# Strassen's scheme for six of seven feature blocks of a spatial product

## The chip, the cores and the metric

The kernel runs on one core of one Trainium2 chip. The metric is device time in microseconds, the median of several executions. The core has five engines with a queue of instructions each: TensorE (PE in the profile, its weight loads PEld), VectorE (DVE), ScalarE (ACT), GpSimd (POOL) and SyncE (SP), which here issues nearly all DMAs.

## The reference

One block of a network: an attention part A, then a gated MLP part B, each with a modulated layer norm ahead and a gated residual behind.

```python
def _B_ref(x, w_in, w_sp, b_sp, w_out):       # x: 1 x 2048 x 448, F = 1792, Fh = 896
    z = _gelu(jnp.einsum('bsd,df->bsf', x, w_in))
    z1 = z[..., :Fh].copy()
    z2 = _layernorm(z[..., Fh:], axis=-1)
    g = jnp.einsum('ts,bsf->btf', w_sp, z2) + b_sp[None, :, None]    # w_sp: 2048 x 2048
    return jnp.einsum('bsf,fd->bsd', z1 * g, w_out)
...
h = _layernorm(x, axis=-1) * (1 + ca) + sa
x = x + ga * _A_ref(h, A_wqkv, A_w_phi, A_wo)
h = _layernorm(x, axis=-1) * (1 + cb) + sb
x = x + gb * _B_ref(h, B_w_in, B_w_sp, B_b_sp, B_w_out)
```

The change concerns the product `w_sp @ z2`, a 2048 x 2048 by 2048 x 896 product, called the spatial product here. Inputs and outputs are bf16; matmuls add up in f32.

## The kernel before

The kernel is a list of small steps. A string, `ORDER`, names them one after the other, and a loop at the end of `fast_path` calls each. Each engine works through its own instructions in that order; nothing rearranges them, so the order by hand sets every queue. A word such as `gM:0,3@A2` calls the step `gM` with arguments 0 and 3 and gives it the PSUM slot A2; `zN:15/G` gives `zN` the engine GpSimd (V is VectorE, S ScalarE, Y SyncE). A second path, `general_path`, is taken only for extreme inputs, by a flag that `guard` computes; it does not run here.

PSUM has eight banks. Before the change they are five slots of a pool: A0, A1 and A2 of two banks, B0 and B1 of one.

The sequence has 2048 rows, 16 tiles (`NT`) of 128. The 896 features are seven blocks of 128 (`FC`). The steps of the last third, around the change:

- `zM` (matmul, L990), `zG` (gelu on ScalarE, L994), `zQ` (squares), `zR` and `zW` (moments, inverse root), `zN` (L1012) make the normalised `z2n`, sequence on the partitions, features in the free dimension.
- `yM` (matmul, L1018) and `yG` (gelu on ScalarE, L1021) make `z1T`, features on the partitions, for a chunk of 512 rows and one feature block.
- `W` (L1026) loads one eighth of a chunk of `w_sp`, transposed by DMA, issued on SyncE. Four chunks of 512 output rows each; their buffers are `wsp0`, the two halves of `EQ` (before that the attention's exponentials) and `hT` (before that the transposed hidden rows).
- `gM` (L1034) is the spatial product: for a chunk and a feature block, 16 matmuls with a 128 x 128 tile of `z2n` as weights and a slice of the chunk as the moving operand, into one bank. The last chunk is cut in two, of 384 and 128 columns:

```python
CH = [(0, 0, 512), (1, 0, 512), (2, 0, 512), (3, 0, 384), (3, 384, 512)]
```

- `gG` (L1040, L1041) takes the bank on VectorE: it adds the bias into an f32 buffer, then multiplies with `z1T` in place.
- `oM` (L1047) is the output product of one tile of 128 rows, seven matmuls over the feature blocks; `oE` (L1050) adds the residual; `oD` (L1053) issues the output DMA on SyncE.
- `wts` (L907) scales a block of `w_out` by the gate, on GpSimd. `guard` (L1056 to L1062) reduces two tables for the flag.

In `ORDER` the 35 units of `gM` stand in line from the last `yM` on; four `yM` and the `oM` of finished chunks stand among them.

Of the kernel before, what the change touches and what calls it, by code (L numbers as in the profile page):

```python
# [515 lines left out]
W:1,7 yG:3,6 gM:0,2@B0 W:1,5 yG:1,6 gG:0,5 gM:0,4@A1 gG:0,2 gG:0,3 yM:2,6@B0 gG:0,4 gM:0,6@A2 yG:2,6 wts:5/G yM:1,3@B0 gG:0,6 gM:0,1@A1 gM:1,4@A2
gM:1,1@A0 gG:1,4 wts:3/G gG:0,0 W:2,0 gM:1,0@A2 yG:1,3 gG:1,1 gM:1,5@B0 W:2,7 gG:1,0 gM:1,6@B1 gG:1,5 gG:0,1 gM:1,2@B0 gG:1,6 wts:4/G W:2,4 W:2,5
wts:6/G gM:1,3@B1 gG:1,2 gM:2,2@B0 gG:1,3 guard@A2 oM:4,0,7@B1 gG:2,2 gM:2,4@A2 oM:1,0,7@B0 oM:0,0,7@A1 oM:5,0,7@A0 oE:0 oE:1 gM:2,1@A1 oD:0/Y gG:2,4
oD:1/Y oM:2,0,7@B0 oM:3,0,7@A2 oE:2 oD:2/Y oM:7,0,7@B0 oE:3 oE:4 oD:3/Y yM:2,1@A2 oE:5 oD:4/Y oD:5/Y yM:2,3@B1 yG:2,1 gM:2,0@A0 gG:2,1 yG:2,3 W:3,6
W:3,7 W:3,0 oM:6,0,7@B1 gG:2,0 W:3,3 gM:2,5@A2 oE:6 oE:7 W:3,2 W:3,1 gM:2,6@B0 oD:6/Y gG:2,5 W:3,4 W:3,5 gM:2,3@B1 gG:2,6 gM:3,2@B0 read gG:2,3  # L520
oM:9,0,7@B1 gG:3,2 oM:11,0,7@A2 gM:3,3@B0 gM:3,4@A1 gG:3,3 gM:3,5@B0 gG:3,4 gM:3,6@A1 gG:3,5 oM:8,0,7@B0 gG:3,6 gM:3,1@A0 oE:8 oE:9 oD:8/Y oD:9/Y
gM:3,0@B0 gG:3,1 oD:7/Y gM:4,6@B1 gG:3,0 gM:4,3@A1 gG:4,6 oM:13,0,7@B0 gG:4,3 gM:4,0@B1 gM:4,5@A1 gG:4,0 gM:4,1@A0 gG:4,5 oM:10,0,7@B1 gG:4,1
gM:4,2@A1 oE:10 oE:11 oM:12,0,7@A0 oD:10/Y gG:4,2 oD:11/Y gM:4,4@B1 hint oE:12 oE:13 oM:14,0,7@A2 oD:12/Y gG:4,4 oD:13/Y oM:15,0,6@B0 oE:14 oD:14/Y
oM:15,6,7@B0 oE:15 oD:15/Y
"""


def fast_path(tc, A_x, A_wqkv, A_w_phi, A_wo, B_w_in, B_w_sp, B_b_sp, B_w_out, c, w_mod, out, flag):
# [525 lines left out]

    def guard(slot):
        nc.vector.tensor_reduce(out=flg[:, 0:1], in_=ksum[:].rearrange("p i a h -> p (i a h)"), axis=AX.X, op=ALU.max)  # L1056
# [96 lines left out]
```

## Time and profile before

| | us |
|---|---|
| median of 3 runs | 266.69 |
| lowest and highest run | 265.77, 266.75 |
| span of the profiled execution, first to last instruction | 264.7 |
| the spatial product's stage in it, first gM matmul to the last oM | 138.75 to 260.62 |

The span is that of one profiled execution. That execution's own time is not listed apart; the span is 2.0 us below the median, which is what lies around it in a run. A row of a group gives line, engine, operation, output and inputs, shapes, count, then busy time, mean duration of one in ns, and the idle time of the engine just before, with what ended it. A row of the timeline begins with the start in us from the first instruction and the duration.

### The profile page before, as it was taken

The numbers are of one execution on the slowest core, as the hardware profiler recorded it, in microseconds if no ns is written. First come the engines' busy times: TensorE is split into PE (matmuls) and PEld (weight loads), VectorE is DVE, ScalarE is ACT, GpSimd is POOL, SyncE is SP. The second block draws the span as 40 slices with busy tenths as digits, with TensorE's granted clock in tenths as the row PEclk, the third lists the DMA queues.
The fourth block names the chain that finished last, engine by engine and source line by source line (L and its number), as shares of the span: only waits on it lengthen the run. The fifth ranks groups of instructions, "written<-read, shape, count | busy, mean of one in ns | idle before, by whom it ended". The sixth has DMA issues, their size and how long they took to land.

```text
span 264.7 us, 4376 instructions
## 1 busy us (share of the span) xinstructions
PE 255.1 (96%) x1645; PEld 138.4 (52%) x1653; DVE 159.1 (60%) x389; ACT 113.1 (43%) x238; POOL 67.5 (26%) x93
## 2 busy tenths in 40 slices
PE   7899999999699999989999999999999999999993
PEld 5764566665445555545444444444444444555771
DVE  5799999966987978867610262435623534335562
ACT  2689978759859998889772000000000100000000
POOL 6328672368623543223362000000000000000000
PEclk9999999999989999999999999999999999999998
DMA  7994999700599431891892000000001398000012
GB/s 179 276 278 102 170 240 276 226 2 20 109 171 156 105 80 40 177 144 41 184 166 49 0 0 0 2 0 0 0 5 35 99 189 120 0 0 23 32 38 78
DMA packets 68656, 25.23 MB, mean 95 GB/s; under 512 B 58129, under 2 KB 68498, under 8 KB 68626
## 3 DMA queue, kind: packets, MB, share of 16 engines
q1 hardware_dynamic: 67088, 22.72, 42.6%
q10 hardware_dynamic: 1538, 2.15, 3.2%
q8 instruction: 15, 0.25, 0.4%
q14 instruction: 15, 0.12, 0.1%
HBM read 8.87 MB, written 1.84 MB: 40 GB/s over the span
## 4 chain that ended last, share of the span: by engine, by line
PE 84%; ACT 5%; DVE 5%; DMA 3%; issue 1%; ACTq 0%; DVEq 0%
PE g_ps L1034 36%; PE o_ps L1047 8%; PE z_ps L990 7%; PE z_ps L1018 7%; PE q_ps L890 5%; PE k_ps L842 4%; PE v_ps L850 4%; PE x_ps L950 4%; PE kvacc L873 3%; PE num L918 2%; DMA f_oT<-f_opad 2%; DMA f_wq_raw<-in_A_wqkv_dram 2%; DVE f_t L934 2%; ACT f_junk L962 1%; PE sh_ps L758 1%
## 5 line engine op out<-in xcount | busy, mean ns | idle before, releaser
L1034 PEld LDWEIGHTS <-f_z2n 128*128 128x128 bf16 x560 | 50.4, 98 | 47.7
L1040 DVE TENSOR_TENSOR f_gb<-g_ps,f_bsp 128x512 f32<-128x512 f32 (+2 forms) x35 | 20.4, 582 | 58.9 <-PE g_ps L1034 58.7
L1034 PE MATMUL g_ps<-f_Eq,f_z2n 128*128 128x512 bf16 x219 | 48.7, 379 | 0.3
L1021 ACT ACTIVATE f_z1T<-z_ps 128x512 bf16<-128x512 f32 x28 | 16.2, 596 | 71.9 <-PE z_ps L1018 71.8
L1018 PE MATMUL z_ps<-f_hT,f_win 113*128 113x512 bf16 (+1 forms) x112 | 26.4, 379 | 0.0
L990 PE MATMUL z_ps<-f_win,f_hT 112*128 112x448 bf16 (+1 forms) x128 | 26.1, 352 | 0.0
L1034 PE MATMUL g_ps<-f_hT,f_z2n 128*128 128x384 bf16 (+1 forms) x224 | 25.4, 272 | 0.0
L1034 PE MATMUL g_ps<-f_wsp,f_z2n 128*128 128x512 bf16 x109 | 24.5, 379 | 0.2
L1047 PE MATMUL o_ps<-f_wout,f_z1T 128*128 128x448 bf16 x112 | 22.8, 353 | 0.0
L1041 DVE TENSOR_TENSOR f_z1T<-f_gb,f_z1T 128x512 bf16<-128x512 f32 (+2 forms) x35 | 20.5, 585 | 1.9 <-ACT f_z1T L1021 0.5
L990 PEld LDWEIGHTS <-f_hT 112*128 112x128 bf16 (+1 forms) x128 | 12.3, 97 | 11.8
L856 DVE TENSOR_REDUCE f_ksum<-f_E 128x32 f32<-128x896 bf16 x16 | 16.8, 1067 | 0.8 <-ACT f_E L845 0.6
L1018 PEld LDWEIGHTS <-f_win 113*128 113x128 bf16 (+1 forms) x112 | 10.7, 97 | 12.3
L1050 DVE TENSOR_TENSOR f_xpad<-o_ps,f_x 128x448 bf16<-128x448 f32 x16 | 9.3, 619 | 13.0 <-PE o_ps L1047 12.5
L895 ACT ACTIVATE f_Eq<-q_ps 112x1024 bf16<-112x1024 f32 x16 | 16.0, 1034 | 2.7 <-PE q_ps L890 2.7
L934 DVE TENSOR_TENSOR f_t<-num,f_w 128x896 bf16<-128x896 f32 x16 | 16.7, 1083 | 0.2
L994 ACT ACTIVATE f_z2g<-z_ps 128x896 bf16<-128x896 f32 x16 | 14.6, 914 | 3.6 <-PE z_ps L990 3.5
L845 ACT ACTIVATE f_E<-k_ps 128x448 bf16<-128x448 f32 x32 | 15.4, 555 | 1.6 <-PE k_ps L842 0.9
L950 PE MATMUL x_ps<-f_wo,f_oT 112*128 112x448 bf16 x64 | 15.5, 372 | 0.7 <-DMA f_oT<-f_opad 0.7
L1047 PEld LDWEIGHTS <-f_z1T 128*128 128x128 bf16 x112 | 10.7, 98 | 9.4
L890 PE MATMUL q_ps<-f_hT,f_Wq 113*128 113x512 bf16 (+1 forms) x64 | 14.9, 378 | 0.0
L842 PE MATMUL k_ps<-f_Wk,f_hT 113*128 113x448 bf16 (+1 forms) x64 | 14.1, 352 | 0.0
(157 smaller groups left out, 337.8 us busy)
## 6 DMA issues: line engine op xcount, KB each, us to landing
out_dram<-f_xpad SPq DMA_DIRECT2D x16, 112.0 KB, 1.7
f_x<-in_A_x_dram SPq DMA_DIRECT2D x3, 448.0 KB, 9.6
f_wm<-in_w_mod_dram SPq DMA_DIRECT2D x3, 406.0 KB, 6.3
f_wout<-in_B_w_out_dram SPq DMA_DIRECT2D x1, 784.0 KB, 7.7
f_wmg<-in_w_mod_dram SPq DMA_DIRECT2D x2, 392.0 KB, 5.0
f_win<-in_B_w_in_dram SPq DMA_DIRECT2D x1, 784.0 KB, 8.3
f_win<-in_B_w_in_dram ACTq DMA_DIRECT2D x1, 784.0 KB, 8.9
f_bsp<-in_B_b_sp_dram ACTq DMA_DIRECT2D x1, 512.0 KB, 5.3
```

The lines of the kernel that those rows point to most:

```text
L842: nc.tensor.matmul(t[:, 0, 0:D], lhsT=hT[0:KR[m], i, m, :], rhs=Wk[0:KR[m], m, :], start=(m == 0), stop=(m == KC - 1))
L856: nc.vector.tensor_reduce(out=ksum[:, i], in_=Er[i % NR][:].rearrange("p s (c f h) -> p (s c) h f", c=4, h=HP), axis=AX.X, op=ALU.add)
L890: nc.tensor.matmul(t[:, u, :], lhsT=Wq[0:KR[m], m, cc * CB:cc * CB + P], rhs=hT[0:KR[m], 4 * st:4 * st + 4, m, :], start=(m == 0), stop=(m ...
L934: nc.vector.tensor_tensor(out=tr[i % 2][:], in0=numv(i)[:, :, :, 0:DH], in1=wr[i // 2 % 2][:, i % 2].unsqueeze(3).to_broadcast([P, 2, H, D ...
L950: nc.tensor.matmul(t[:, 0, 0:D], lhsT=oT[0:CB, i % 4, cc, :], rhs=wo_s[0:CB, cc, :], start=(cc == 0 and not with_x), stop=(cc == KC - 1))
L990: nc.tensor.matmul(t[:, hf, 0:D], lhsT=hT[0:KR[m], i, m, :], rhs=win_s[0:KR[m], m, FH + hf * D:FH + (hf + 1) * D], start=(m == 0), stop=(m ...
L1018: nc.tensor.matmul(t[:, 0, :], lhsT=win_s[0:KR[m], m, fc * P:(fc + 1) * P], rhs=hT[0:KR[m], 4 * st:4 * st + 4, m, :], start=(m == 0), stop ...
L1021: nc.scalar.activation(out=stage_b()["z1T"][:, fc, st * 512:(st + 1) * 512], in_=ps["y%d_%d" % (st, fc)][:, 0, :], func=ACT.Gelu_apprx_tanh)
L1034: nc.tensor.matmul(g[:, 0, 0:b - a], lhsT=later["z2n"][:, s_, fc * P:(fc + 1) * P], rhs=wspT[t][:, s_, a:b], start=(s_ == 0), stop=(s_ == ...
L1040: nc.vector.tensor_tensor(out=gb, in0=ps["G%d_%d" % (ch, fc)][:, 0, 0:b - a], in1=bsp[:, t * TCHF + a:t * TCHF + b], op=ALU.add)
L1041: nc.vector.tensor_tensor(out=z, in0=gb, in1=z, op=ALU.mult)
L1047: nc.tensor.matmul(ps["o" + str(t)][:, 0, 0:D], lhsT=later["z1T"][:, fc, t * P:(t + 1) * P], rhs=wout_s[:, fc, :], start=(fc == 0), stop=( ...
```

## The change

For feature blocks 0 to 5 the spatial product is computed by one level of Strassen's scheme (in Winograd's form). The 2 x 2 blocks are: of `w_sp`, two chunks of 512 output rows by two halves of the sequence (A); of `z2n`, two halves of the sequence by two groups of three feature blocks (B). For each of two pairs of chunks, `p`, and each of three block pairs, `f`, seven products of eight matmuls take the place of eight. Feature block 6 keeps `gM` and `gG`.

New steps:

- `tT` (VectorE, bf16, 128 x 768): the four differences of the B blocks, in quarters, 16 in all. Three go into new views, one over `z2n` itself.
- `sS` (VectorE, bf16, 128 x 2048): the four sums of the A blocks of a pair, in halves, 16 in all.
- `pM`: one product, eight matmuls over 512 columns into one bank. Products 2, 3 and 4 add onto the bank of an earlier one (2 on 1, 4 on 7, 3 on 5), after that has been read.
- `pc` (ScalarE) copies product 1 out; `pb` (GpSimd, two operations) adds the two bias rows to it; `uB`, `uA`, `uW`, `cA` (VectorE, 128 x 512, a bank plus an f32 buffer or the bias) build the four result blocks; `cX` (VectorE or GpSimd) multiplies a result with `z1T` in place.

Moved: chunk 1's `W` loads go where chunk 2's stood; chunk 2 is loaded into the memory of `win_s` and `wo_s` after the last `yM`; chunk 3 into chunk 1's buffer, issued after products 4 of pair 0 have been issued. Four `yM`, the four late `wts` and `zN:15` (now on VectorE) come ahead of the first `gM`. Eight `oM` stand between products 2 and 6 of pair 1; the other eight at the end. `guard` gives its matmul to a new step `guard2`. PSUM is one tile of eight banks, and a slot is a view of it; several SBUF tiles (`win_s` and `wo_s`, `opad` and `oT`, `junk` and `junk2`, the `f_t` and `f_z2g` rings) become views of one tile each.

```diff
+tT:1,0,2/V tT:2,0,2/V tT:3,0,2/V tT:4,0,2/V zQ:12/S yM:1,6@A1 zQ:13/V zM:14@A0 yG:2,0 zR:12,14 ...
+tT:1,2,4/V ... tT:4,2,4/V yM:3,5@A2 W:1,5 yG:1,6 yG:3,6 yG:3,2 yM:2,2@A0 zR:14,16 yG:3,5 yM:3,0@B1 zW:14,16 yG:2,2 zN:14/V zN:15/V
+yM:3,1@A2 ... yG:2,3 wts:5/G wts:3/G wts:4/G wts:6/G W:2,0 W:2,1 W:2,2 W:2,3 W:2,4 W:2,5 W:2,6 W:2,7
+gM:0,6@3 sS:0,1,0/V sS:0,2,0/V gM:1,6@7 sS:0,1,1/V sS:0,2,1/V pM:0,0,1@6 pc:0,0 pb:0,0 gG:0,6 pM:0,1,1@5 pc:0,1 pb:0,1 gG:1,6 pM:0,0,2@6 sS:0,3,0/V
+sS:0,3,1/V pM:0,2,1@1 pc:0,2 pb:0,2 cA:0,0,11 pM:0,1,2@5 cX:0,0,11/G pM:0,2,2@1 cA:0,1,11 cX:0,1,11/G cA:0,2,11 cX:0,2,11/G pM:0,0,6@0 uB:0,0 uA:0,0
+pM:0,0,7@2 uW:0,0 pM:0,1,6@4 uB:0,1 uA:0,1 pM:0,0,4@2 cA:0,0,21 pM:0,1,7@3 uW:0,1 sS:0,4,0/V cX:0,0,21/G pM:0,2,6@7 uB:0,2 uA:0,2 pM:0,1,4@3 cA:0,1,21
...
+sS:1,2,1/V oM:2,0,7@0 oE:2 oD:2/Y sS:1,3,0/V oM:3,0,7@4 oE:3 oD:3/Y sS:1,3,1/V oM:4,0,7@3 oE:4 oD:4/Y oM:5,0,7@6 oE:5 oD:5/Y oM:6,0,7@0 oE:6 oD:6/Y
+oM:7,0,7@4 oE:7 oD:7/Y sS:1,4,0/V pM:1,0,6@0 uB:1,0 uA:1,0 pM:1,0,7@2 uW:1,0 pM:1,1,6@4 uB:1,1 uA:1,1 pM:1,0,4@2 cA:1,0,21 pM:1,1,7@3 uW:1,1
...
+    psum = psp.tile([P, 8, 512], F32, name="f_psum")
+    SLOT = {"A0": (0, 2), "A1": (2, 4), "A2": (4, 6), "B0": (6, 7), "B1": (7, 8)}
+    SLOT.update({str(k): (k, k + 1) for k in range(8)})
     def bank(slot, name):
-        if slot[0] == "A":
-            return psp.tile([P, 2, 512], F32, name=name, tag=slot, bufs=1)
-        return psp.tile([P, 1, 512], F32, name=name, tag=slot, bufs=1)
+        a, b = SLOT[slot]
+        return psum[:, a:b, :]
...
-    wspT = [wsp0[:], EQ[:, 0, :].rearrange("p (n t) -> p n t", t=TCHF), EQ[:, 1, :].rearrange("p (n t) -> p n t", t=TCHF),
-            hT[:].rearrange("p n k t -> p n (k t)")]
+    wspT = [wsp0[:], EQ[:, 0, :].rearrange("p (n t) -> p n t", t=TCHF), wbig[:, 0:NT * TCHF].rearrange("p (n t) -> p n t", t=TCHF),
+            EQ[:, 0, :].rearrange("p (n t) -> p n t", t=TCHF)]
...
+    def tT(k, a, b, eng):
+        z = [[zblk(s, g)[:, a:b] for g in range(2)] for s in range(2)]
+        t1, t2, t4 = [TS[u][:, a:b] for u in range(3)]
+        out_, in0, in1 = {1: (t1, z[0][1], z[0][0]), 2: (t2, z[1][1], t1), 3: (z[0][1], z[1][1], z[0][1]), 4: (t4, z[1][0], t2)}[k]
+        eng.tensor_tensor(out=out_, in0=in0, in1=in1, op=ALU.subtract)
...
+    def sS(p, k, h, eng):
+        A, S = [[v[:, :, h * 256:(h + 1) * 256] for v in w] for w in wblk(p)]
+        out_, in0, in1, op = {1: (S[0], A[2], A[3], ALU.add), 2: (S[1], S[0], A[0], ALU.subtract),
+                              3: (S[2], A[0], A[2], ALU.subtract), 4: (S[3], A[1], S[1], ALU.subtract)}[k]
+        eng.tensor_tensor(out=out_, in0=in0, in1=in1, op=op)
+    PSTART = {1: True, 2: False, 3: False, 4: False, 5: True, 6: True, 7: True}
+    def pM(p, f, k, slot):
+        A, S = wblk(p)
+        a = {1: A[0], 2: A[1], 3: S[3], 4: A[3], 5: S[0], 6: S[1], 7: S[2]}[k]
+        b = {1: zblk(0, 0), 2: zblk(1, 0), 3: zblk(1, 1), 4: TS[2], 5: TS[0], 6: TS[1], 7: zblk(0, 1)}[k]
+        t = ps["P%d_%d_%d" % (p, f, k)] = bank(slot, "p_ps")
+        for j in range(NH):
+            nc.tensor.matmul(t[:, 0, :], lhsT=b[:, j, f * P:(f + 1) * P], rhs=a[:, j, :], start=(PSTART[k] and j == 0), stop=(j == NH - 1),
+                             skip_group_check=True)
...
+    def pc(p, f):
+        nc.scalar.copy(out=slotA(f), in_=pP(p, f, 1))
+    def pb(p, f):
+        nc.gpsimd.tensor_tensor(out=slotB(f), in0=slotA(f), in1=bias(p, 1), op=ALU.add)
+        nc.gpsimd.tensor_tensor(out=slotA(f), in0=slotA(f), in1=bias(p, 0), op=ALU.add)
+    def vadd(out_, bank_, other):
+        nc.vector.tensor_tensor(out=out_, in0=bank_, in1=other, op=ALU.add)
+    def uB(p, f):
+        vadd(slotB(f), pP(p, f, 6), slotB(f))
+    def uA(p, f):
+        vadd(slotA(f), pP(p, f, 6), slotA(f))
+    def uW(p, f):
+        vadd(slotC(f), pP(p, f, 7), slotB(f))
...
```

More of the change, by code (lines that the diff above doesn't have):

```diff
@@ L516 @@
[L516 to L523, printed above, removed]
@@ L549, in fast_path @@
     hT = persist.tile([P, NT, KC, P], BF, name="f_hT")
-    win_s = persist.tile([P, KC, 2 * FH], BF, name="f_win")
-    wo_s = persist.tile([P, KC, D], BF, name="f_wo")
+    wbig = persist.tile([P, KC * (2 * FH + D)], BF, name="f_win")
+    win_s = wbig[:, 0:KC * 2 * FH].rearrange("p (k n) -> p k n", k=KC)
+    wo_s = wbig[:, KC * 2 * FH:].rearrange("p (k n) -> p k n", k=KC)
     wout_s = persist.tile([P, FC, D], BF, name="f_wout")
@@ L559, in fast_path @@
     xpad = persist.tile([P, NX, KC, P], BF, name="f_xpad")
-    opad = persist.tile([P, NO, KC, P], BF, name="f_opad")
+    oo = persist.tile([P, 2 * NO * KC * P], BF, name="f_oo")
+    opad, oT = [oo[:, u * NO * KC * P:(u + 1) * NO * KC * P].rearrange("p (t k e) -> p t k e", t=NO, k=KC) for u in range(2)]
     wsp0 = persist.tile([P, NT, TCHF], BF, name="f_wsp0")
@@ L1004, in stage_b @@
             later["z1T"] = zp.tile([P, FC, S], BF, name="f_z1T")
-            later["z2g"] = [zp.tile([P, 2, D], BF, name=f"f_z2g{r}") for r in range(NZ)]
+            zt = zp.tile([P, NZ * FH], BF, name="f_z2g")
+            later["z2g"] = [zt[:, r * FH:(r + 1) * FH].rearrange("p (a d) -> p a d", a=2) for r in range(NZ)]
+            tmps.extend(f32v(zt[:, u * 1024:(u + 1) * 1024]) for u in range(4))
             later["gb"] = [zp.tile([P, TCHF], F32, name=f"f_gb{r}") for r in range(2)]
@@ L1053, in oD, with zblk @@
         eng.dma_start(out=outv[t], in_=later["ot"][t % NX])
-    def guard(slot):
+    def zblk(s, g):
+        return later["z2n"][:, s * NH:(s + 1) * NH, g * FB:(g + 1) * FB]
+    def tT(k, a, b, eng):
[3 more added lines that the diff above has]
+        eng.tensor_tensor(out=out_, in0=in0, in1=in1, op=ALU.subtract)
@@ new lines, in vadd, with cA @@
+    def vadd(out_, bank_, other):
[6 more added lines that the diff above has]
+        vadd(slotC(f), pP(p, f, 7), slotB(f))
+    def cA(p, f, k):
+        if k == 11:
+            vadd(later["gb"][f % 2][:], pP(p, f, 2), bias(p, 0))
+        elif k == 21:
+            vadd(slotB(f), pP(p, f, 4), slotB(f))
+        elif k == 22:
+            vadd(slotC(f), pP(p, f, 5), slotC(f))
+        else:
+            vadd(slotA(f), pP(p, f, 3), slotA(f))
@@ L1056, in guard, with cX @@
+    def cX(p, f, k, eng):
+        src = {11: lambda: later["gb"][f % 2][:], 21: lambda: slotB(f), 22: lambda: slotC(f), 12: lambda: slotA(f)}[k]()
+        fc, t = f + (3 if k % 10 == 2 else 0), 2 * p + (k // 10 - 1)
+        z = later["z1T"][:, fc, t * TCHF:(t + 1) * TCHF]
+        eng.tensor_tensor(out=z, in0=src, in1=z, op=ALU.mult)
+    def guard():
         nc.vector.tensor_reduce(out=flg[:, 0:1], in_=ksum[:].rearrange("p i a h -> p (i a h)"), axis=AX.X, op=ALU.max)
```

62 lines of the change are left out of this document (50 added, 12 removed).

## The prediction

> **What bounds the kernel now.** I read the page first: who is busy, and whether the clock is full.
>
> ```profile
> PE 255.1 (96%) x1645; PEld 138.4 (52%) x1653; DVE 159.1 (60%) x389; ACT 113.1 (43%) x238; POOL 67.5 (26%) x93
> ...
> PEclk9999999999989999999999999999999999999998
> ```
>
> TensorE is the bound by share. An average over stages does not say what a change in one stage is worth, so next the table by stretches, for the spatial product (columns: stretch, length, then busy us and count of PE, PEld, DVE, ACT, POOL; clock; DMA share; GB/s).
>
> ```profile
> 170.00:180.00 10.00, 9.95 (x47) 4.47 (x46) 5.17 (x9) 0.00 (x0) 0.00 (x0) 1.00 0.00 0
> ...
> 220.00:230.00 10.00, 10.00 (x53) 5.07 (x52) 3.97 (x7) 0.00 (x0) 0.00 (x0) 1.00 0.39 49
> ```
>
> In the stage PE never waits, at full clock; DVE is half idle, ACT and POOL wholly. So here every matmul removed shortens the run, until one of the others is late. The chain of waits in order of time (start, us, what) gives the price of one matmul as chain time, the pipeline overlap taken out:
>
> ```profile
> 131.81 6.94 PE z_ps L1018 x32
> 138.75 0.22 PE g_ps L1034
> ...
> 156.88 3.46 PE g_ps L1034 x16
> ...
> 230.79 10.40 PE g_ps L1034 x64
> ...
> 250.82 2.68 PE g_ps L1034 x48
> ...
> 257.94 2.66 PE o_ps L1047 x14
> ...
> 260.62 0.62 DVE f_xpad L1050
> ```
>
> A matmul over 512 columns costs 3.46/16 = 0.216 us, over 384 columns 10.40/64 = 0.1625, over 128 columns 2.68/48 = 0.056, an o_ps one 2.66/14 = 0.19. The spatial stage runs from 138.75 to 260.62 with no gap.
>
> **PE: what goes.** Before, gM makes 21 units of 16 at 512, 7 of 16 at 384 and 7 of 16 at 128 columns (L1028 splits the last chunk). After, feature block 6 alone keeps gM: 3, 1 and 1 units. The six other blocks are 2 chunk pairs x 3 block pairs x 7 products x 8 = 336 matmuls at 512. So 512-column matmuls go from 336 to 336 + 48, the narrower ones from 112 to 16 each: +48 x 0.216 - 96 x 0.1625 - 96 x 0.056 = 10.4 - 15.6 - 5.3 = -10.6 us (48 of 384 full-width equivalents, one eighth). The o_ps and z_ps matmuls are the same, four yM only stand earlier. If nothing waits, the span of 264.7 becomes 254.1.
>
> **What DVE gets.** Rows of the groups by form (engine, operation, out<-in, count | busy, mean ns | idle before):
>
> ```profile
> L1041 DVE TENSOR_TENSOR f_z1T<-f_gb,f_z1T 128x512 bf16<-128x512 f32 x21 | 14.5, 692 | 1.4 <-ACT f_z1T L1021 0.5
> L1040 DVE TENSOR_TENSOR f_gb<-g_ps,f_bsp 128x512 f32<-128x512 f32 x21 | 14.5, 689 | 44.2 <-PE g_ps L1034 44.1
> L1050 DVE TENSOR_TENSOR f_xpad<-o_ps,f_x 128x448 bf16<-128x448 f32 x16 | 9.3, 619 | 13.0 <-PE o_ps L1047 12.5 <-DMA out_dram<-f_xpad 0.5
> L863 DVE TENSOR_TENSOR f_phik<-f_E,f_kr 128x896 bf16<-128x896 bf16 x12 | 7.2, 627 | 0.1
> L964 DVE SCALAR_TENSOR_TENSOR f_junk<-f_z2g 128x896 bf16<-128x896 bf16 x4 | 4.3, 1086 | 1.1 <-ACT f_z2g L994 1.1
> L907 DVE TENSOR_TENSOR f_wout<-f_wout,f_g_rep 128x448 bf16<-128x448 bf16 x1 | 0.4, 384 | 0.0
> L907 POOL TENSOR_TENSOR f_wout<-f_wout,f_g_rep 128x448 bf16<-128x448 bf16 x6 | 6.1, 1028 | 0.0
> L863 POOL TENSOR_TENSOR f_phik<-f_E,f_kr 128x896 bf16<-128x896 bf16 x4 | 7.1, 1779 | 9.1 <-DVE f_kr L860 8.4 <-ACT f_Eq L895 0.7
> L1056 DVE TENSOR_REDUCE f_flg<-f_ksum 128x1 f32<-128x512 f32 x1 | 0.7, 680 | 0.0
> ```
>
> L907 and L863 on DVE give bf16 tensor_tensor a slope of (627-384)/448 = 0.54 ns per element; L964, another operation with two bf16 inputs, takes 1086 ns for 896, twice that slope. The new operations are plain tensor_tensor, so I take the first: sS, 2048 elements, 627 + 1152 x 0.54 = 1.25 us; tT, 768 elements, 0.56. The other end is L964's: 1.09 + 1152 x 1.04 ns = 2.3 and 0.95. Each evacuation (uA, uB, uW, cA) has the form of L1040, each cX on DVE that of L1041: 0.69, with the gap 0.73. On POOL 512 elements cost, between its rows, 1.14 us.
>
> Now the two queues side by side, because the products accumulate on banks that DVE reads in between, so a late DVE stops PE within a product or two.
>
> ```profile
> 133.83 1.21 ACT L1021 ACTIVATE f_z1T<-z_ps 128x512 bf16<-128x512 f32 x2
> 135.13 0.51 DVE L1012 TENSOR_SCALAR f_z2n<-f_z2g,f_zm,f_zv 128x896 bf16<-128x896 bf16 x1 [0.81 <-POOL f_zv L976]
> ...
> 149.15 0.69 DVE L1040 TENSOR_TENSOR f_gb<-g_ps,f_bsp 128x512 f32<-128x512 f32 x1 [13.50 <-PE g_ps L1034]
> ```
>
> Lead-in (timeline). DVE ends its last normalisation at 135.6 and idles 13.5 us. The 16 tT (9 us) go there and into its smaller gaps before, half of them ahead of the statistics of the last tiles: these eight are 4.7 us with gaps, and as some fall into idle time I put the last zN 3.4 later, near 139 (at most at 140.3), and the last tT 4.7 on, near 143.7. PE starts gM at 138.75 + four yM of 0.867 = 142.2, and I add 0.7: yG:1,6 and yG:3,6 now stand ahead of yG:3,2 on ACT, which ends at 133.83 + 3 x 0.60 = 135.6, while yM:3,0, which wants its bank, is due at 131.81 + 4 x 0.867 = 135.3, plus the hand-over (0.3 to 1.0). So PE starts at 142.9 and last wants zN:15 3 us later: covered.
>
> Pair 0, first part. PE: two gM and six products of 8 matmuls (1.73 each), 6.9 + 10.4, to 160.2; then product 6, which needs sS:1 and sS:2, product 7 with sS:3. DVE from 143.7: four sS 5.1, two gG 2.9, two sS 2.5: S2 is ready at 149, S3 at 154. Covered by 8 us and more. Second part: 15 products, 25.9 us on PE. DVE: 18 evacuations 13.1, six cX 4.4, two sS 2.5, guard 1.9 (two reductions like L1056 and three small ones) = 21.9. Fits, 4 us to spare. Product 4 goes onto product 7's bank and waits for uW, with one product between: 0 to 1.2, I take 0.3, as DVE has slack.
>
> Pair 1, first part. PE: six products 10.4 and eight oM 10.6 = 21. DVE: six sS 7.6, three cA 2.2, eight oE 5.2 = 15. The sS wait for chunk 3, whose DMAs stand on SP behind the last read of chunk 1:
>
> ```profile
> 209.51 8.03 SPq L1026 DMA_TRANSPOSE f_hT<-in_B_w_sp_dram  x6
> ...
> f_hT<-in_B_w_sp_dram SPq DMA_TRANSPOSE x8, 3.8
> ```
>
> Six issues take 8.03, so 1.34 each, landing 3.8 after issue; five products (8.7 us) lie between that read and pair 1. The first four have landed 3 x 1.34 + 3.8 = 7.8 us on, all eight after 13.2, 4.5 us into pair 1: early enough, and the output DMAs behind them on SP lose nothing that PE wants. Chunk 2, into the former win_s, has all of pair 0. Four of the oM have an sS beside their oE, 1.9 us of DVE for 1.32 of PE: 2.4 us behind; the next three oM regain 0.67 each, so oE:6, whose bank product 6 wants, is late by some 0.6 (0 to 2.4). Second part as in pair 0: 13.1 + seven cX 5.1 + two sS 2.5 + two oE 1.3 = 22 of 25.9. POOL has 23 operations of 1.14, 26 us of 90, and ACT six copies; the four wts moved ahead are hidden there. The end (last oM, oE, DMA) is unchanged.
>
> **The sum.** -10.6 + 0.7 + 0.3 + 0.6 and 0.5 for POOL meeting DVE (below) = -8.5. The span goes to 256.2. The time of the profiled execution itself is not listed; its span is 2.0 below the median of the runs, 266.69, so I carry the difference over: 258.2 us. The views of banks and tiles move no work; the built program has 27 more semaphore instructions on DVE and 18 on ACT. Such a one takes 21 ns:
>
> ```profile
> L907 DVEq EVENT_SEMAPHORE  x1: 21/21/21, 55.2 to 55.2; - x1
> ```
>
> All of DVE's on the path would be 27 x 0.021 = 0.6 us; beside the slack above I count none.
>
> **Rivals.** *A: POOL holds DVE.* Where they met:
>
> ```profile
> 54.73 3.16 POOL L907 TENSOR_TENSOR f_wo<-f_wo,f_g_rep 112x448 bf16<-112x448 bf16 x3 [4.31 <-ACT f_g_rep L904]
> ...
> 55.31 0.70 DVE L907 TENSOR_TENSOR f_wo<-f_wo,f_g_rep 112x448 bf16<-112x448 bf16 x1
> ...
> L940 DVE TENSOR_TENSOR f_opad<-f_t x11: 379/382/625, 69.2 to 111.4; 128x448 bf16<-128x448 bf16 x11
> ```
>
> Under POOL's run the DVE operation took 0.70 against 0.384, and the longest of L940 0.625 against 0.382: 0.2 to 0.3 us for one meeting. In the forecast most of these fall into slack. If instead DVE lost the whole POOL operation, then in pair 1's first part nine of them add up to 10.3 to DVE's 15 against PE's 21: 4.3 late, and some 1.5 in each second part, where 3 or 2 are left (22 + 3.4 = 25.4 of 25.9): 7.3 in place of 0.5, 265.0. The Trainium skill, SBUF — State Buffer, "Who interferes with whom", says that a DVE instruction with two SBUF inputs contends with a GpSimd one that reads SBUF and the later one fully blocks; by that rule it would be this case. The trace agrees that they meet, and shows less than a full block.
>
> *B: DVE becomes the bound*, on the slower side. If sS and tT run at L964's slope, 16 x 1.05 + 16 x 0.39 = 23 us more on DVE. Pair 0: the last tT at 150, S3 at 150 + 9.2 + 2.9 + 4.6 = 167 where PE wants it at 161.9: 5 late, and the three cA behind it make the first uB, uA, uW late by 1.5 more. Pair 1's first part then holds 15 + 6.3 = 21.3 plus the wait for chunk 3 against 21, with the oE in step behind an sS of 2.3: 4 to 5 late, and the second parts (24 of 25.9) have nothing left to win back. 5 + 1.5 + 4.5 and the 2.1 above are 13: 266.7 - 10.6 + 13 = 269, slower. It decides where an sS takes over about 2 us. Against it: L863 and L907 are the same operation.
>
> *C: it doesn't save what it says*, because the products wait for each other in the bank chain 6-7-4, one product of 1.73 apart: half of the 1.2 above, 0.6, for each of the six times that a product 4 follows a product 7, is 3.6 in place of 0.3: 261.5, inside the range.
>
> **Chances.** Forecast 0.62 (256.1, with no waits, to 260.5), C 0.10, A 0.12, B 0.12, anything else 0.04. A change under 0.5% (1.3 us) can't be told from none. Of A, 0.06 stays faster, 0.05 is the same and 0.01 slower; of the rest half is faster. Faster: 0.62 + 0.10 + 0.06 + 0.02 = 0.80; same 0.05; slower: 0.12 + 0.01 + 0.02 = 0.15. The range runs from 255.8 (no waits, less a little spread) to 265.0, A's price; B, the upper half of A and half of the rest are left out, 0.20.
>
> **What would show it.** Right: 336 product matmuls at 0.216 in the chain, over 95% PE from the first gM to the end, sS at 1.25, DVE busy 75 to 85% in the stage, end of PE near 252. Wrong: PE waiting on the evacuations for over 5 us in total, sS rows over 1.6 (A or B, by whether a POOL row lies beside them), or PE idle ahead of the first product.

## The result and the profile after

The changed kernel takes 258.06 us (median of four runs, 257.26 to 258.41) against 266.23 for the kernel before, a ratio of 0.969 (95% interval 0.966 to 0.972): 8.2 us, 3.1%, faster. The forecast was 258.2. A second set of runs gave 257.63 against 266.24, 0.967 (0.963 to 0.970).

The head of the page and the clock row, after:

```profile
PE 243.3 (95%) x1501; PEld 127.2 (50%) x1509; DVE 193.9 (76%) x417; ACT 116.9 (46%) x244; POOL 98.1 (38%) x115
...
PEclk9999999999999999999999999999999999999999
```

1501 matmul records in place of 1645; PE is still the bound, with 95% of a shorter span. VectorE has gone from 60% to 76%. The chain of waits in order of time (start, us, what) shows the stage:

```profile
135.95 7.10 PE f_psum L1042 x32
143.05 0.22 PE f_psum L1058
...
196.80 10.59 PE f_psum L1071 x56
...
242.96 7.96 PE f_psum L1071 x42
250.94 0.62 DVE f_xpad L1074
```

From the first gM at 143.05 to the last oM at 250.94 the chain stays on PE; one matmul of `guard2` and some gaps of 0.05 us stand among the products. That is 107.9 us. Before, the same work took 260.62 - 138.75 - 3.47 (the four yM that have moved) = 118.4. The difference is 10.5 us, the 10.6 of the prediction. The first gM starts 0.85 later than its counterpart before (142.2), and 4.5 us of the span lie behind the start of the last residual addition where 4.1 did: -10.5 + 0.85 + 0.4 is the 9.3 by which the two profiled spans differ (264.7, 255.4). The profiled execution of the second set spans 256.0 us, 8.7 less than before. Single executions of one kernel differ by a microsecond or more, so the medians' 8.2 and the profiles' 9.3 are not at odds. In the second set the 168 matmuls of the products up to the guard are one row, 36.27 us, 0.216 us for a matmul:

```profile
150.33 36.27 PE f_psum L1109 x168
```

The table by stretches, cut at the parts of the two pairs (length, busy us and count of PE, PEld, DVE, ACT, POOL; clock; DMA share; GB/s):

```profile
138.75:160.00 21.25, 21.14 (x98) 9.64 (x99) 19.13 (x21) 5.34 (x9) 10.43 (x8) 1.00 0.58 100
160.00:186.00 26.00, 25.89 (x120) 11.69 (x120) 18.65 (x29) 0.00 (x0) 9.33 (x8) 1.00 0.34 62
186.00:208.00 22.00, 21.89 (x109) 10.57 (x110) 15.44 (x21) 1.76 (x3) 12.07 (x9) 1.00 0.23 56
208.00:234.00 26.00, 25.89 (x120) 11.81 (x121) 18.36 (x27) 0.00 (x0) 2.32 (x2) 1.00 0.03 10
```

PE is full in every part; VectorE is idle for 2.1, 7.4, 6.6 and 7.6 us of them. But VectorE's rows are not those that were priced. The sums `sS`, by source line (count, then min/median/max in ns, first and last start), and GpSimd beside two of them (timeline):

```profile
L1098 DVE TENSOR_TENSOR f_hT<-f_hT,f_wsp x2: 1225/1226/1226, 146.3 to 148.7; 128x2048 bf16<-128x2048 bf16 x2
L1098 DVE TENSOR_TENSOR f_Eq<-f_wsp,f_Eq x2: 2173/2176/2180, 152.8 to 154.9; 128x2048 bf16<-128x2048 bf16 x2
L1098 DVE TENSOR_TENSOR f_hT<-f_hT,f_win x2: 1215/1428/1642, 192.3 to 200.7; 128x2048 bf16<-128x2048 bf16 x2
```

```profile
152.38 1.52 POOL L1132 TENSOR_TENSOR f_t<-f_Eq,f_bsp 128x512 f32<-128x512 f32 x1 [10.67 <-ACT f_Eq L1129]
153.98 2.02 POOL L1133 TENSOR_TENSOR f_Eq<-f_Eq,f_bsp 128x512 f32<-128x512 f32 x1
155.96 2.14 POOL L1132 TENSOR_TENSOR f_junk<-f_Eq,f_bsp 128x512 f32<-128x512 f32 x1
159.29 1.15 POOL L1132 TENSOR_TENSOR f_z2g<-f_oo,f_bsp 128x512 f32<-128x512 f32 x1
```

Alone an sS takes 1.22 us; two that meet `pb` on GpSimd take 2.18. GpSimd's operations, 1.15 alone (the last row), take 1.5 to 2.1 there. So both are held up, far more than the 0.2 to 0.3 us for a meeting that the prediction allowed, and the run does not show it. The experiments ask why.

### The profile page after: what moved, and what is told of

It reads as the page before. It is cut to its first block, busy times and chain, and to the rows that moved or that the text cites. A ratio compares the mean times of both kernels' runs of the same rounds, so it can differ in the third digit from the quotient of the medians.

```text
span 255.4 us, 4195 instructions
## 1 busy us (share of the span) xinstructions
PE 243.3 (95%) x1501; PEld 127.2 (50%) x1509; DVE 193.9 (76%) x417; ACT 116.9 (46%) x244; POOL 98.1 (38%) x115
## 4 chain that ended last, share of the span: by engine, by line
PE 81%; DMA 5%; ACT 4%; DVE 4%; issue 2%; POOL 1%; SPq 1%; DVEq 0%; POOLq 0%; ACTq 0%
PE f_psum L1109 28%; PE f_psum L1071 8%; PE f_psum L1012 8%; PE f_psum L1042 7%; PE f_psum L1058 5%; PE f_psum L864 5%; PE f_psum L872 4%; PE f_psum L912 3%; DMA f_hT<-f_xpad 3%; PE f_psum L972 3%; PE f_psum L895 3%; DMA f_oo<-f_oo 2%; PE f_psum L726 2%; PE f_psum L940 1%; DVE f_t L956 1%
## 5 line engine op out<-in xcount | busy, mean ns | idle before, releaser
L1109 PEld LDWEIGHTS <-f_z2n 128*128 128x128 bf16 x192 | 18.7, 98 | 22.4
L1012 PE MATMUL f_psum<-f_win,f_hT 112*128 112x448 bf16 (+1 forms) x128 | 26.3, 352 | 1.0 <-DMA f_hT<-f_xpad 1.0
L1109 PE MATMUL f_psum<-f_wsp,f_z2n 128*128 128x512 bf16 x119 | 27.2, 379 | 0.1
L1042 PE MATMUL f_psum<-f_hT,f_win 113*128 113x512 bf16 (+1 forms) x112 | 26.1, 378 | 0.2 <-ACT f_z1T L1045 0.2
L1109 PE MATMUL f_psum<-f_hT,f_Eq 128*128 128x512 bf16 x92 | 22.3, 379 | 0.2
L1071 PE MATMUL f_psum<-f_wout,f_z1T 128*128 128x448 bf16 x112 | 21.7, 352 | 0.0
L1045 ACT ACTIVATE f_z1T<-f_psum 128x512 bf16<-128x512 f32 x28 | 16.0, 597 | 4.5 <-PE f_psum L1042 4.4
L917 ACT ACTIVATE f_Eq<-f_psum 112x1024 bf16<-112x1024 f32 x16 | 16.0, 1035 | 2.7 <-PE f_psum L912 2.7
L956 DVE TENSOR_TENSOR f_t<-f_psum,f_w 128x896 bf16<-128x896 f32 x16 | 16.7, 1084 | 0.2
L867 ACT ACTIVATE f_E<-f_psum 128x448 bf16<-128x448 f32 x32 | 15.4, 555 | 1.8 <-PE f_psum L864 0.9
```

The costliest lines, as they stand in the source:

```text
L867: nc.scalar.activation(out=Er[i % NR][:, s, :], in_=ps["k" + str(i)][:, 0, 0:D], func=ACT.Exp, scale=1.0 - 2.0 * s)
L917: nc.scalar.activation(out=Eq[st // 2][0:CB, 2 * c2:2 * c2 + 2, s, (st % 2) * 512:(st % 2 + 1) * 512], in_=ps["q" + str(n)][0:CB, :, :], f ...
L956: nc.vector.tensor_tensor(out=tr[i % 2][:], in0=numv(i)[:, :, :, 0:DH], in1=wr[i // 2 % 2][:, i % 2].unsqueeze(3).to_broadcast([P, 2, H, D ...
L1012: nc.tensor.matmul(t[:, hf, 0:D], lhsT=hT[0:KR[m], i, m, :], rhs=win_s[0:KR[m], m, FH + hf * D:FH + (hf + 1) * D], start=(m == 0), stop=(m ...
L1042: nc.tensor.matmul(t[:, 0, :], lhsT=win_s[0:KR[m], m, fc * P:(fc + 1) * P], rhs=hT[0:KR[m], 4 * st:4 * st + 4, m, :], start=(m == 0), stop ...
L1045: nc.scalar.activation(out=stage_b()["z1T"][:, fc, st * 512:(st + 1) * 512], in_=ps["y%d_%d" % (st, fc)][:, 0, :], func=ACT.Gelu_apprx_tanh)
```

## Experiments

**Theory:** the gain is the removed matmul slots and nothing else, and the new work lies in slack. **Rivals:** a part of the gain comes from the new storage or order; VectorE is near to being the bound (B); GpSimd's hold on VectorE is paid for (A). Ratios are to the kernel before, run beside each.

### Storage alone

The kernel before with all the views and merged tiles, its order and its weight buffers unchanged; and the kernel before with the PSUM views alone:

```diff
     def bank(slot, name):
-        if slot[0] == "A":
-            return psp.tile([P, 2, 512], F32, name=name, tag=slot, bufs=1)
-        return psp.tile([P, 1, 512], F32, name=name, tag=slot, bufs=1)
+        a, b = SLOT[slot]
+        return psum[:, a:b, :]
```

> The kernel before with the storage part of the change alone: PSUM banks as views of one tile, and the buffers f_win/f_wo, f_opad/f_oT, f_junk, f_t and f_z2g each merged to one tile; order of work, weight chunks and products are those of before. Theory (the gain is the removed matmul slots): the same as before, 266.2 us within 0.7. Rival (a part of the gain comes from the new storage, through waits between banks that the pools kept and the views do not): 1 to 4 us faster, with the PE's waits in the product shorter.

> The kernel before with the PSUM banks as views of one tile and nothing else. With the merged SBUF tiles as well it took 267.3 us against 266.1, a ratio of 1.006. Theory V (the views of the banks cost it, through the waits that the scheduler sets between bank users): ratio 1.004 to 1.009. Rival T (the merged tiles cost it, those of the attention output and of its transpose above all, whose DMA the PE waited for 0.9 in place of 0.7 us): ratio within 0.998 to 1.002.

Measured: all the storage 267.33 us, ratio 1.0057 (1.0026 to 1.0089); the PSUM views alone 266.43, 1.0031 (1.0007 to 1.0055). No part of the gain comes from here; on the contrary, the storage costs 0.7 to 2.4 us, and at least a part of that comes with the PSUM views: their ratio lies below what theory V expected and above what rival T did. The two intervals overlap, so the times alone do not say how much the merged SBUF tiles add. One place where the traces differ lies about 20 us ahead of the stage. First the kernel before, then the one with PSUM views alone (PE's timeline, and the DMA table around the issue, median us from issue to landing):

```profile
119.04 6.25 PE L990 MATMUL z_ps<-f_win,f_hT 113*128 113x448 bf16 x32
...
f_hT<-f_xpad SPq DMA_TRANSPOSE x1, 2.8
```

```profile
121.53 3.21 PE L994 MATMUL f_psum<-f_win,f_hT 113*128 113x448 bf16 x16 [0.51 <-DMA f_hT<-f_xpad]
...
f_hT<-f_xpad SPq DMA_TRANSPOSE x1, 3.8
```

The transpose T3:12,14 lands 3.8 us after its issue in place of 2.8, and PE, which ran 32 matmuls in one row before, waits 0.5 us for it in the middle. The wait is there in the changed kernel too, 0.5 at 122.59 us. In all ten traces of kernels that have the views and issue T3 at this place it lands after 3.7 to 3.8 us; the pool's tiles have one trace.

The merged tiles show at other transposes, above all at that of the attention output, whose buffers `opad` and `oT` became one tile. First the PSUM views alone, then all the storage (PE's timeline):

```profile
115.41 0.93 PE L954 MATMUL f_psum<-f_wo,f_oT 112*128 112x448 bf16 x4 [0.45 <-DMA f_oT<-f_opad]
```

```profile
116.63 0.93 PE L956 MATMUL f_psum<-f_win,f_oo 112*128 112x448 bf16 x4 [0.90 <-DMA f_oo<-f_oo]
```

Over the four waits for transposes from 77 to 123 us PE loses 1.6 us with the PSUM views alone and 2.4 with all the storage. These 0.8 us would be what the merged tiles add; they rest on one trace of each kernel, and no run has the merged tiles alone.

### The changed kernel without Strassen

No tT and no sS; chunks 0 to 3 as plain units, in the changed kernel's buffers and lead-in:

```diff
-sS:0,1,0/V sS:0,2,0/V ... pM:0,0,1@6 pc:0,0 pb:0,0 ... pM:0,2,3@7 cA:0,2,12 cX:0,2,12/V guard2@3
+gM:1,0@6 gG:1,0 gM:1,1@5 gG:1,1 ... gM:0,4@1 gG:0,4 gM:0,5@0 gG:0,5 guard2@3
```

> The changed kernel without Strassen: storage, weight buffers and order of the lead-in of the changed kernel, no tT and no sS, and the six feature blocks of chunks 0 to 3 as plain products (24 groups of 16 matmuls with 512 columns in place of 42 groups of 8). 48 matmuls more at 0.216 us are 10.4 us. Theory: 258.1 + 10.4 less the 1.0 us that the tT cost in the lead-in = 267.5 us (266.3 to 268.5), and the PE again without waits in the stage. Rival (a part of the gain comes from order, buffers or the chunk that is no longer split): below 265.

Measured: 268.51 us, ratio 1.0104 (1.004 to 1.017), 10.45 us above the changed kernel by the medians and 11.1 by the ratios, good to some 1.7 us; 48 matmuls of 0.216 are 10.4. The traces are sharper: from the first gM to the last oM this kernel takes 118.2 us (142.66 to 260.82), the changed kernel 107.9, and PE is without a wait in both. So Strassen's scheme itself brings all that its matmul slots are worth, and the rest of the change costs: it makes the kernel some 2.4 us slower than before by the medians (1.1 to 4.5 by the interval), of which the storage above is about half. None of that lies in the stage, which took 118.4 us before. The tT, expected to cost 1.0 us of the lead-in, cost nothing. PE's last wait ahead of the stage is there without them, first this kernel, then the changed one:

```profile
135.56 7.10 PE L1051 MATMUL f_psum<-f_hT,f_win 113*128 113x512 bf16 x32 [0.16 <-ACT f_z1T L1054]
```

```profile
135.95 7.10 PE L1042 MATMUL f_psum<-f_hT,f_win 113*128 113x512 bf16 x32 [0.16 <-ACT f_z1T L1045]
```

### Strassen in pair 0 only

```diff
-pM:1,0,1@1 pc:1,0 pb:1,0 ... pM:1,2,3@7 cA:1,2,12 cX:1,2,12/V
+gM:2,0@1 gG:2,0 gM:2,1@5 gG:2,1 ... gM:5,4@1 gG:5,4 gM:5,5@0 gG:5,5
```

> The changed kernel with Strassen in pair 0 (chunks 0 and 1) alone; the six feature blocks of chunks 2 and 3 are plain products. T3 stands in the place of a part of z2n, so the plain products of pair 1 take it as an operand for feature blocks 3 to 5: that part of the output is not the reference's, the work is of the same size. 24 matmuls more at 0.216 us are 5.2 us. Theory: each pair saves by its own matmuls and nothing else, 258.1 + 5.2 = 263.3 us (262.6 to 264.0). Rival (one pair brings most of it, as pair 1 hides what pair 0 cannot, or the other way round): under 261 or over 265.

Measured: 262.86 us, ratio 0.988 (0.982 to 0.994), between 268.51 and 258.06: the first pair brings 5.65, the second 4.80, and 24 slots are 5.2. The interval is some 1.6 us to either side, so the two pairs cannot be told apart. Within that the gain goes by slots, pair by pair.

### A slower sS: rival B's point

```diff
-        eng.tensor_tensor(out=out_, in0=in0, in1=in1, op=op)
+        eng.scalar_tensor_tensor(out=out_, in0=in0, scalar=1.0, in1=in1, op0=ALU.mult, op1=op)
```

> The changed kernel with the 16 weight combinations sS as scalar_tensor_tensor (operand 0 times 1.0, then plus or minus operand 1) in place of tensor_tensor; values are the same. The form is expected to cost VectorE the prediction's other end, 2.3 us each, about 17 us more in all. Rival B as the prediction worked it out: VectorE becomes the bound, 258.1 + 9 to 11 = 267 to 269 us. Theory (VectorE has 2.1, 7.4, 6.6 and 7.6 us idle in the four parts of the stage of the changed kernel): the 8.6 us more in each pair stand against 9.5 and 14.2 us of idle time, so the PE waits where S2, S3 or an evacuation comes late, 0 to 4 us: 258 to 262 us. If the form costs no more than tensor_tensor, the time is 258.1 and the run tells nothing.

Measured: 269.22 us, ratio 1.012 (1.005 to 1.018), 11.2 us more. Rival B it is, and the theory of slack by whole parts fell. The groups by form (mean ns, then idle before), and PE's timeline where it waited, in the profiled execution, with 271.60 us the longest of the four:

```profile
L1098 DVE SCALAR_TENSOR_TENSOR f_hT<-f_Eq 128x2048 bf16<-128x2048 bf16 x4 | 9.1, 2280 | 0.0
L1098 DVE SCALAR_TENSOR_TENSOR f_Eq<-f_wsp,f_Eq 128x2048 bf16<-128x2048 bf16 x2 | 6.4, 3242 | 0.0
```

```profile
160.85 1.89 PE L1109 MATMUL f_psum<-f_hT,f_Eq 128*128 128x512 bf16 x8
164.61 1.89 PE L1109 MATMUL f_psum<-f_Eq,f_z2n 128*128 128x512 bf16 x8 [1.87 <-DVE f_Eq L1098]
...
170.49 2.66 PE L1109 MATMUL f_psum<-f_Eq,f_oo 128*128 128x512 bf16 x8 [2.27 <-DVE f_z2g L1136]
172.94 2.85 PE L1109 MATMUL f_psum<-f_Eq,f_z2n 128*128 128x512 bf16 x8
...
183.37 1.89 PE L1109 MATMUL f_psum<-f_Eq,f_oo 128*128 128x512 bf16 x8 [0.67 <-DVE f_z2g L1136]
...
215.61 1.48 PE L1071 MATMUL f_psum<-f_wout,f_z1T 128*128 128x448 bf16 x7 [1.68 <-DVE f_xpad L1074]
219.83 3.27 PE L1109 MATMUL f_psum<-f_hT,f_Eq 128*128 128x512 bf16 x8 [2.74 <-DVE f_xpad L1074]
```

An sS takes 2.28 us alone and 3.24 beside GpSimd. S3 comes late (1.87), the evacuations behind it too (2.27, 0.67), and in pair 1 the oE that stand between the sS (1.68, 2.74): 9.2 us of waits. A stall can be paid twice: eight product matmuls take 1.89 in this view, but 2.66 and 2.85 after the second wait and 3.27 after the last, 3.1 us more. The table by stretches shows the granted clock (the column after the engines'):

```profile
168.20:170.50 2.30, 0.04 (x2) 0.01 (x1) 2.30 (x5) 0.00 (x0) 1.95 (x2) 1.00 0.00 0
171.50:174.50 3.00, 3.00 (x9) 1.06 (x7) 0.82 (x2) 0.00 (x0) 0.54 (x1) 0.50 0.00 0
175.00:177.00 2.00, 2.00 (x11) 0.94 (x10) 1.17 (x2) 0.00 (x0) 0.11 (x1) 1.00 0.00 0
```

PE idles for 2.3 us, and a microsecond later it gets half its clock for 3.4 us (171.5 to 174.9 by finer stretches); after the last wait it is as long again. The other three executions, of 268.58 to 269.80 us, have a mean granted clock of 0.984 to 0.989 where this one has 0.976, so they lost less to it.

### No GpSimd in the product stage

```diff
     def pb(p, f):
-        nc.gpsimd.tensor_tensor(out=slotB(f), in0=slotA(f), in1=bias(p, 1), op=ALU.add)
-        nc.gpsimd.tensor_tensor(out=slotA(f), in0=slotA(f), in1=bias(p, 0), op=ALU.add)
+        nc.scalar.copy(out=slotB(f), in_=pP(p, f, 1))
...
-cX:0,0,11/G ... cX:1,2,22/G
```

> The changed kernel with GpSimd taken out of the product stage: pb (the two bias additions for each of six feature blocks) becomes one copy on ScalarE without the bias, and the 11 or so cX that stood on GpSimd are left out, so the bias of the first product and the gating of those blocks are missing from the output. Theory (VectorE and GpSimd do hold each other up, but inside VectorE's slack): the two sS at 2.18 us fall to 1.22, those at 1.52 to 1.64 too, VectorE's busy time in the stage falls by 3 to 5 us, and the time stays at 258.1 us within 0.7. Rival A (the meeting with GpSimd is paid for by the run): 2 us faster or more, 256 or below.

Measured: 257.14 us, ratio 0.968 (0.963 to 0.973, 1.3 us to either side), where the changed kernel has 0.969. The sS that met `pb` are down at 1.22, so GpSimd was what held them:

```profile
L1098 DVE TENSOR_TENSOR f_Eq<-f_wsp,f_Eq x2: 1219/1220/1221, 152.6 to 153.8; 128x2048 bf16<-128x2048 bf16 x2
```

The meeting is real, and the run does not pay for it. Rival A's mechanism is there; its price, 7 us, is not, and not because of slack alone. VectorE's busy time in the stage (143 to 251 us) falls by 2.0 us only, from 75.7 to 73.6, where 3 to 5 were expected; in the first part of pair 1, where A counted 10.3 us of meetings, it falls by 0.4. In this order few operations meet.

### More load on VectorE

A tensor_tensor of 0.65 us behind the evacuations of every product of the second parts (15 in each pair), and of every other product (8 and 7). The cut shows the first:

```diff
+    def dv():
+        nc.vector.tensor_tensor(out=KVbd[:].rearrange("p s c h d -> p (s c h d)"), in0=bsp[:, 0:960], in1=bsp[:, 960:1920], op=ALU.add)
...
-uB:0,0 uA:0,0 pM:0,0,7@2 uW:0,0 pM:0,1,6@4 uB:0,1 uA:0,1 ...
+uB:0,0 uA:0,0 dv pM:0,0,7@2 uW:0,0 dv pM:0,1,6@4 uB:0,1 uA:0,1 dv ...
```

> The changed kernel with a plain tensor_tensor of 960 bf16 elements (from the bias row into a dead tile) put on VectorE behind each evacuation of the second parts, 15 in each pair, about 0.66 us each, 9.9 us for a pair; the result is not touched. The second parts leave VectorE 7.4 and 7.6 us idle. Slack theory (all of the idle time of a part can be used): the PE waits for 2.5 + 2.3, so 258.1 + 4.8 = 262.9 us (261.5 to 264). Rival (only the slack between neighbouring products can be used, as the banks let VectorE lag by one product at most): two thirds or more of the 19.8 us are paid, 271 us and above. Third case (VectorE has no part in it): 258.1.

> As with 15 operations behind the evacuations of each second part, but 7 or 8, behind every other one: 5 us a pair against 7.4 and 7.6 us of idle time. With 15 the run took 3.9 us more. Slack theory: all of it fits, 258.1 us within 0.7. Rival (a half of the load costs a half): 260.0 us.

Measured: with 15, 261.95 us, ratio 0.984 (0.979 to 0.990), 3.9 us more than the changed kernel's first set; with 7 or 8, 260.94, 0.981 (0.976 to 0.987), 3.3 more than its second set, which ran beside it. By the ratios the two loads cost 4.1 and 3.9 us, so these runs do not tell a half of the load from all of it. The first is near the slack theory's sum, but not for its reason, and the second is against it: a load that fits the idle time is paid for. Where PE waited, with 15, then with half of them:

```profile
166.43 1.89 PE L1128 MATMUL f_psum<-f_Eq,f_oo 128*128 128x512 bf16 x8 [0.80 <-DVE f_z2g L1155]
...
178.22 1.89 PE L1128 MATMUL f_psum<-f_Eq,f_oo 128*128 128x512 bf16 x8 [1.27 <-DVE f_z2g L1155]
...
188.03 1.89 PE L1128 MATMUL f_psum<-f_wsp,f_z2n 128*128 128x512 bf16 x8 [1.01 <-DVE f_z2g L1155]
```

```profile
165.46 1.89 PE L1127 MATMUL f_psum<-f_Eq,f_oo 128*128 128x512 bf16 x8 [0.80 <-DVE f_z2g L1154]
...
176.61 1.89 PE L1127 MATMUL f_psum<-f_Eq,f_oo 128*128 128x512 bf16 x8 [0.63 <-DVE f_z2g L1154]
```

All listed waits are in pair 0. The first is that of product 4 for uW:0,0, the bank chain of the prediction, and the second is the same for uW:0,2. How near the first was in the changed kernel, its timelines of VectorE and of PE say:

```profile
162.82 0.69 DVE L1136 TENSOR_TENSOR f_gb<-f_psum,f_bsp 128x512 f32<-128x512 f32 x1 [3.50 <-POOL f_z1T L1161]
...
164.63 0.68 DVE L1136 TENSOR_TENSOR f_z2g<-f_psum,f_t 128x512 f32<-128x512 f32 x1
```

```profile
165.36 1.89 PE L1109 MATMUL f_psum<-f_Eq,f_oo 128*128 128x512 bf16 x8
```

uW:0,0 ends at 165.31, and product 4 starts at 165.36, 0.05 us behind it. That is the distance at which PE starts where it did wait (166.38 and 166.43 with 15 operations), so no margin is left, and one operation of 0.65 (0.91 there, as it met GpSimd) put ahead of uW is paid for. VectorE had sat idle for 3.5 us until 162.82, since the two `gb` buffers wait for a cX, which stands behind six `pb` on GpSimd. So the idle time of a part is not the slack of its first operations.

Ahead of the second wait GpSimd's hold is paid for. With half the load, the sS in front of uW:0,2 takes 2.18 us, as it comes behind a cX on GpSimd (173.38 to 174.88), and PE then waits 0.63 us. In the changed kernel the same sS came first and took 1.22, and the cX took 2.07.

```profile
173.78 2.18 DVE L1116 TENSOR_TENSOR f_wsp<-f_wsp,f_hT 128x2048 bf16<-128x2048 bf16 x1
```

In pair 1 the 15 operations cost 0.1 us. Nothing of the kind stands there ahead of the first evacuation, which is the likely reason. The 120 matmuls of its second part, with 15 and in the changed kernel's second set:

```profile
211.15 26.06 PE f_psum L1128 x120
```

```profile
207.76 25.96 PE f_psum L1109 x120
```

With half the load, the waits above explain 1.4 of the 3.3 us. Its profiled execution also has 6.0 us behind the start of its last VectorE operation, where the changed kernel's two have 4.5 and 4.7, which no run explains.

### The lead-in

```diff
-wR:14/V zQ:9/S wM:15@A0 l2a:13/V l2a:12/V
+l2a:13/V l2a:12/V wR:14/V zQ:9/S wM:15@A0
...
-yG:1,6 yG:3,6 yG:3,2 yM:2,2@A0
+yG:3,2 yG:1,6 yG:3,6 yM:2,2@A0
```

> The changed kernel with two moves in the lead-in: the normalisations l2a:13 and l2a:12 go ahead of wR:14 on VectorE, where it sat idle from 115.2 to 117.5 us, so that the transpose DMA T3:12,14 starts 1 to 1.5 us sooner; and yG:3,2 goes ahead of yG:1,6 and yG:3,6 on ScalarE. In the trace of the changed kernel the PE waited 0.5 us for that DMA and 0.2 to 0.3 for that yG. Theory: 0.5 to 0.8 us faster than the changed kernel, 257.4 us. Rival (the next wait, for the normalisation of the z rows or for the last yG, takes the place of these): 258.1.

> The changed kernel as it is, beside the two versions with other lead-ins, so that they stand on one chip: ratio 0.969 to the kernel before, 258 us.

> The lead-in with l2a:13, l2a:12 and yG:3,2 moved, a second time beside the changed kernel. Theory: both waits stay away and the gain of 0.5 to 0.8 us shows, a ratio about 0.003 below that of the changed kernel. Rival: the 257 us of the first time were spread, and the two ratios agree within 0.001.

Measured: first 256.94 us, ratio 0.967 (0.962 to 0.972); the second time 256.36, 0.961 (0.957 to 0.964), beside 257.63, 0.967 (0.963 to 0.970), for the changed kernel: 1.1 and 1.3 us less by the medians, 0.5 and 1.5 by the ratios. The intervals of the second comparison overlap a little, so the size is loose. In the first trace T3 starts at 116.89 us and the first gM at 142.52, 0.9 earlier than in the changed kernel's second trace, and both waits have gone from the list; from 100 us to the stage only this is left:

```profile
116.95 0.93 PE L989 MATMUL f_psum<-f_win,f_oo 112*128 112x448 bf16 x4 [0.95 <-DMA f_oo<-f_oo]
```

A further move was aimed at that row: nM:15 ahead of yM:1,2, with yM:1,2 now behind yM:1,4.

> That version with one more move: nM:15 ahead of yM:1,2 on the PE (into the bank pair A1, with A1 and A2 exchanged from there to the end of the lead-in) and its nX and nC earlier on ScalarE and VectorE, so that the last transpose of the attention output starts some 0.7 us sooner; in the trace the PE waited 0.95 us for that DMA at 116.95 us. Theory: 0.7 us below the version without it, 256.3 us. Rival (another wait in the lead-in, for the next bank or the normalisation, takes its place): no change, or up to 0.5 us slower.

Measured: 256.96 us, ratio 0.965 (0.961 to 0.968), no gain over the version without it. In this order zM:7 writes the bank of yM:1,2 ahead of yG:1,2's read, so one block of z1T in it is not the reference's. The wait for the DMA fell to 0.54. Another of 0.98 stands at 81 us, and it need not come from the move: this trace has no half-clock stretch at 72 us (see the last section), and the changed kernel's trace without one also waits 1.0 us at that place (0.46 and 0.54). The version with the first two moves has the lowest median of all.

## Why the prediction was right, point by point

- **PE, -10.6 us.** Right. The stage is 10.5 shorter than before and 10.3 shorter than without Strassen, and one pair is worth about a half.
- **Durations on VectorE.** sS 1.22 (1.25), tT 0.55 (0.56), an evacuation 0.68 to 0.69 (0.69); on GpSimd 1.15 (1.14). All hold for an operation alone. The two sS that met GpSimd made S3 ready at 157.1 in place of 154, still 4.8 us ahead of its product. The choice of the tensor_tensor rows over L964's slope carried the forecast: at 2.28 us the run takes 269.2, which is rival B's 269. Its waits of 5 + 1.5 in pair 0 were 4.8, its 4 to 5 in pair 1 were 4.4; the slower tT, which it counted, were not in this run, and the half clock, 3.1 us in the profiled execution, was not in its sum. That the totals agree is in part luck.
- **Lead-in, +0.7.** The size is near (0.85 in the first trace, 1.2 in the second), the cause was not all there. The yG in the way cost 0.2 to 0.3; another 0.5 is the wait for T3, which comes with the storage.
- **"The views of banks and tiles move no work", at 0.** This step failed. By the ratios they cost 0.8 us (PSUM views alone) and 1.5 (all). Of that the wait for T3 is 0.5, and longer waits for other transposes are some 0.8 by one trace of each version. Why the storage makes PE wait for them stays open.
- **Stalls in the stage: 0.3 for product 4, 0.6 for oE:6, 0.5 for GpSimd.** All three were zero. Product 4 was right as the nearest limit: it had no margin left. For oE:6, 56 oM in 10.59 us leave no room for a wait.
- **GpSimd meeting VectorE, 0.2 to 0.3 each.** Far too little: 0.96. The first row that it was read from was no sign of a weak hold: the VectorE operation at 55.31 began 0.58 us into a GpSimd operation of 1.0 to 1.2 us, so about a half of that was left to lose, and it lost 0.32. Three `pb` (3.45 us alone) and two sS (2.44) were under way together from 152.38 to 158.10, 5.72 us: they took turns. So the rule of the Trainium skill, SBUF — State Buffer, "Who interferes with whom", which the prediction held to be too strong, is borne out: with two SBUF inputs on VectorE the two engines exclude each other. An evacuation, with one input in PSUM, it exempts, and their rows stay at 0.68 to 0.69 us. Rival A's price went wrong by its count of meetings; its 1.5 in each second part did not follow from its own sum either, 25.4 of 25.9.
- **The signs named.** "sS over 1.6 is wrong" was a bad test: 2.18 came, and cost nothing. VectorE busy 75 to 85% of the stage was too high, 70% (75.6 of 107.9 us).

The main term, -10.6, is right for its reason. That the total, -8.5 for -8.2, is so near is luck: 1.4 us of stalls that did not come, and 0.4 us of the yG's price, stand against storage that was not free, 1.5 us by its ratio (0.7 to 2.4). With the measured sizes the sum is -10.5 + 0.3 + 1.5 = -8.7, and no run places the rest.

## What to carry to other kernels

Where PE is full and the other engines have room, removed matmul slots come back one for one, and the price of one slot in the chain is enough to forecast it; but run the plain version in the new buffers and order as well, since the wrapping can cost a quarter of the gain. Slack is a margin at a place, not the idle time of a stage: look up the first operation after a wait on another engine, and whom it feeds. Price an elementwise operation by a row of the same operation and types; here the form with a scalar takes nearly twice as long (2.28 for 1.22 us) and turns the change into a loss.

## What the runs showed of the hardware that was not expected

- In the run with the slower sS, waits of PE of 2.3 and 2.7 us were each followed by 3.4 us at a granted clock of 0.50 (171.5 to 174.9 and 219.3 to 222.7 us). A wait of 1.87 us there, and the waits of 0.8 to 1.3 us in the run with 15 operations, brought no such stretch. The length of the wait does not decide alone. A wait of 1.95 us at about 70 us stands in all 14 traces; in eight of them a stretch of 3.4 us at half clock follows (6.8 in one), in six none does. First the kernel before, then the changed kernel's first trace:

```profile
72.00:75.00 3.00, 3.00 (x14) 1.45 (x12) 2.67 (x12) 0.73 (x3) 0.87 (x2) 0.50 1.02 108
```

```profile
72.00:75.00 3.00, 2.88 (x16) 1.38 (x15) 2.83 (x12) 1.59 (x6) 1.12 (x2) 1.00 1.21 135
```

  In the run with the slower sS the half-clock stretches begin at 72.5, 171.5 and 219.3 us, 29 and 14 times 3.41 us apart. So it may matter where a wait falls on a fixed grid; no run tests that. The Trainium skill, TensorE: Matmul & The Clock Gate, Part 1, gives half rate after an idle window of about 3.4 us, until a busy one has passed. The half rate and its length agree; the waits that brought it here were shorter than that window.
- VectorE and GpSimd took turns: 2.18 us for 1.22 on one, up to 2.14 for 1.15 on the other.
- With PSUM slots as views of one tile, one transpose DMA landed 3.7 to 3.8 us after its issue, in ten traces, where with a pool's tiles it landed after 2.8, in the one trace of that. The cause is open.
